# The decay of the smaller score blocks of pairs 8 to 15: added by VectorE from broadcast rows, in place of a TensorE product

## The chip, the cores and the metric

The kernel runs on one core of a Trainium2 chip. Its time is the device time of one execution in microseconds (us). Three executions of the kernel before took 973.07, 972.63 and 972.79 us, median 972.79. The profile is one more execution, recorded by the hardware profiler; it took 974.05 us by the clock that times the runs, and the span between its first and last instruction is 972.2 us.

The engines run side by side, each through its own list of instructions in order: TensorE (PE, with its weight loads as PEld), VectorE (DVE), ScalarE (ACT), GpSimd (POOL) and SyncE (SP), which here only starts DMA transfers.

## The reference

Attention over 4 batches of 8 heads, 576 positions and 64 dimensions a head, with a bias that decays with the distance of two positions, and then two dense layers with an activation between:

```python
scores = scale * np.matmul(q, k.transpose(0, 1, 3, 2))
causal = np.triu(np.ones((S, S), dtype=bool), k=1)
cum = np.cumsum(np.maximum(s, 0.0), axis=-1)
bias = -(cum[:, :, :, None] - cum[:, :, None, :])
scores = np.where(causal, -1000000000.0, scores + np.minimum(bias, 0.0))
attn = softmax(scores)          # max, exp, sum and divide, by rows
x = attn @ v                    # heads side by side: 2304 x 512
h = x @ w_in;  x = np.maximum(0.01 * h, h) @ w_out
h = x @ w_in2; out = (np.maximum(h, 0) + np.log1p(np.exp(-np.abs(h)))) @ w_out2
```

All of it is fp32. For a query at row i and a key at column j the bias is cum[j] - cum[i]: a value of the key's column less a value of the query's row.

## The kernel before, in words

The 32 heads are worked on as 16 pairs, p = 0 to 15; "the ninth pair" is p = 8. A pair's two heads (j = 0 and 1) lie on SBUF partitions 0 to 63 and 64 to 127, so that the score products of both stand side by side in the PE array. The 576 queries of a head are cut into four blocks of 128, t = 0 to 3, and a tail of 64. Block t sees (t + 1) * 128 keys. A pair is worked through in four units, in this order:

- A: block 3, 512 keys.
- B: the tails of both heads, 288 keys each. It takes its decay from the tile M, which `bias` (L267) has prepared.
- C: block 2, 384 keys.
- D: blocks 1 and 0, 256 and 128 keys.

For A, C and D, `scores` (L286) issues, for each block, a product K,Q and a second product BK,BQ into the same PSUM tile pt_s: BK and BQ hold the running sums, split in two parts, and rows of ones, and their product is the decay (L311). VectorE then reads the PSUM tile, adds the causal mask, and finds the row maximum in the same instruction (`maxima`, L332). ScalarE takes the exponential (L344), VectorE the reciprocal of the row sum (L350, L351), GpSimd multiplies by it (L355), TensorE transposes the result (L363 to L372), and after an evacuation by ScalarE or VectorE (L384, L386) TensorE multiplies by V (`pv`, L404).

The score tiles have the PSUM tags s0 and s1 (one for each head) with two buffers each. Units take the buffers in turn: A, B, C, D, and A of the next pair takes the buffers of C. So the first score products of the next pair wait until VectorE has finished the maxima of C, of head 0 for s0 and of head 1 for s1.

The order of all this is written by hand in one loop over steps n = 4p + i (L467). From p = 7 on (`late`), step i = 0 starts the scores of B and does the two products with V for the earlier pairs, step 2 starts the scores of C and D, step 3 those of the next pair's A. Between them `fill.step` puts pieces of the first dense layer of earlier batches on TensorE, so that it always has work. `later(n, ...)` issues an instruction n ticks on; a step has two ticks.

SyncE starts the transfers of a pair in step i = 0: V (of this pair, as soon as the product with V of p - 2 has read the old one), then Q, K, four small rows for BK and BQ, and the two loads for M of the next pair (`decays`, L253, from the sums c_d in DRAM). DMA transfers signal their end on eight semaphores in turn. A transfer whose semaphore still belongs to an unfinished one is not issued, and as SyncE works in order, nothing behind it is either.

`Fill` (L539 on) also loads and splits the weights of the first layer; raw weights land in the tiles rawi and rawo. After attention, the two dense layers run as one long chain of TensorE products (`ps_h` L145, `ps_out` L772).

Of the kernel before, what the change touches and what calls it, by code (L numbers as in the profile page):

```python
# [10 lines left out]
F32 = mybir.dt.float32  # L11
# [20 lines left out]
def attn_moe_moe(ctx, tc, q, k, v, s, w1i, w1o, w2i, w2o, out):  # L32
# [122 lines left out]
    def attention(att, ps, fills):  # L155
# [9 lines left out]
        M = two("M", [P, S])  # L165
        CQ, CD = (att.tile([P, n], F32, tag=nm, name=nm) for nm, n in (("CQ", 32), ("CD", 2 * TL)))
        V = two("V", [P, NB + 1, 2, D])
# [71 lines left out]
        def load(p, nm, queue=nc.sync, c=slice(None)):  # L239
            if p < NP:  # L240
                t, x = {"q": (Q, q), "k": (K, k), "v": (V, v)}[nm]
                queue.dma_start(t[p % 2][:, c], x[p, :, c])

        def rows(p):

            if p < NP:
                b, hs = heads(p)
                for j in range(2):
                    h, r = b * H + hs.start + j, j * D
                    move(BK[p % 2][r:r + 2], bb_d[h, :, :SB])  # L250
                    move(BQ[p % 2][r + 32:r + 34], bb_d[h, :, :SB])

        def decays(p):  # L253

            if p < NP:
                o = c_d.offset + p * 2 * S
                for j in range(2):
                    nc.sync.dma_start(M[p % 2][j * D:(j + 1) * D], bass.AP(c_d.tensor, o + j * S, [[0, D], [1, S]]))

        def columns():  # L260
            pt = ps.tile([P, 512], F32, tag="m", name="pt_c", bufs=1)
            nc.tensor.transpose(pt[:, :BH], CD[:BH], ident[:BH, :BH])
            for j in range(2):
                r = slice(j * D, (j + 1) * D)
                nc.vector.tensor_copy(CQ[r, :NP], pt[r, j:BH:2])

        def bias(p):  # L267
            if 0 < p < NP:
                m = M[p % 2]
                nc.vector.tensor_scalar(m, m, CQ[:, p:p + 1], None, op0=ALU.subtract)  # L270
                later(1, nc.gpsimd.tensor_tensor, m[:, SB:], m[:, SB:], maskl[:, SH - TL:], ALU.add)


        class Unit:
# [11 lines left out]
            def scores(self):  # L286
                i = self.p % 2
                bq, bk = (BQ[i], BK[i]) if self.p else (BQ0, BK0)
                ops = (Q[i], K[i]), (bq, bk)
                self.ps = [ps.tile([P, 512], F32, tag=f"s{j}", name="pt_s", bufs=2) for j in range(2)]  # L290
# [16 lines left out]
                for t, c in self.subs:  # L307
                    for x, y in ops:
                        for j in range(2):
                            r = slice(j * D, (j + 1) * D)  # L310
                            nc.tensor.matmul(  # L311
                                self.ps[j][:, c], x[r, t * P:(t + 1) * P], y[r, :(t + 1) * P],
                                start=x is Q[i], stop=x is bq,
                            )
# [4 lines left out]
            def maxima(self, j):  # L319
                if j == 0:  # L320
# [4 lines left out]
                w = slice(0, self.W)  # L325
                ml = (mask[:, w], maskl)[j] if not self.p else M[self.p % 2][:, j * SH:(j + 1) * SH]
                todo = [(w, ml, j)] if self.last else [
                    (c, mask[:, (NB - 1 - t) * P:], j * len(self.subs) + i) for i, (t, c) in enumerate(self.subs)
                ]
                low = self.stat(0, 0) if self.last and j else 3.0e38  # L330
                for c, m, e in todo:
# [126 lines left out]
        live = {}  # L458
        wide = 7

# [6 lines left out]
        for n in range(len(units) + 3):  # L467
# [27 lines left out]
            if i == 0:  # L495
                bias(p)
                if p:
                    load(p + 1, "q")
                    load(p + 1, "k")
                    rows(p + 1)  # L500
                    decays(p + 1)
            tick()
# [20 lines left out]
            if u2:  # L523
                if not soon:
                    u2.evacuate(0)
                u2.transpose(1)
            if i == 3 and not late:
                load(p + 1, "v")
# [7 lines left out]
    class Fill:  # L536
        def __init__(self, ps):
# [3 lines left out]
            self.stack = ExitStack()  # L541
            wio["i"] = new("rawi", 2)
            with_o = pool("rawo", 2, side="right")
# [4 lines left out]
            self.loads, self.splits = {}, {}  # L548
            for t, x in zip(at, zip(blocks, "iioiiiii" + "i" * 4)):
                for d, n in zip((self.loads, self.splits), t):  # L550
# [320 lines left out]
```

## Time and profile before

| | |
|---|---|
| Median of three executions | 972.79 us (972.63 to 973.07) |
| The profiled execution | 974.05 us, span 972.2 us |
| Attention | 0 to about 226 us of the span |
| Pairs 8 to 15 | about 105 to 226 us |
| VectorE, ScalarE, GpSimd busy, whole span | 526.8, 537.3, 576.5 us |

TensorE's share is in the rows below. Busy means that an instruction is being executed; a wait for a semaphore is not busy time. A row of the timeline stands for one instruction or for several like ones that follow on each other (x4 and so on); its second number is the time from the first one's start to the last one's end. A K,Q product in fp32 shows as two instructions for each head, so x4 for a pair.

### The profile page before, as it was taken

Reading aid. Unit: us, or ns where it says so; the run is one execution under the profiler, and the core shown is the slowest. Engines: PE = TensorE matmul, PEld = TensorE weight load, DVE = VectorE, ACT = ScalarE, POOL = GpSimd, SP = SyncE. Lnnn points to the kernel's source line nnn. Section 1 sums busy time; section 2 is a strip of 40 time slices with the busy share of each in tenths; the row PEclk is TensorE's granted clock in tenths of the full one; section 3 lists DMA queues with packets and bytes.
Section 4 is the critical chain, followed back from the end, with each engine's and each line's share of the span. In section 5 each row is a group of like instructions: output and inputs, shape, how many; then the busy total and the mean of one; then the engine's idle time right before and its main releaser. Section 6 shows DMA issues by size and latency. Waiting matters only on the chain.

```text
span 972.2 us, 14745 instructions
## 1 busy us (share of the span) xinstructions
PE 963.7 (99%) x5268; PEld 785.5 (81%) x5268; DVE 526.8 (54%) x1140; ACT 537.3 (55%) x1119; POOL 576.5 (59%) x568
## 2 busy tenths in 40 slices
PE   9999999999999999999999999999999999999998
PEld 6666767777988888888888888888888888888886
DVE  7888567553222232222234357667688768764434
ACT  6888677564453333333344457667656655654452
POOL 6778556443454444444445556777677767774554
PEclk9999999999999999999999999999999999999999
DMA  6544433421621111111111110211011201100202
GB/s 227 160 160 135 139 128 103 149 71 48 224 69 44 44 44 43 44 44 44 44 31 57 44 44 23 66 43 44 23 46 45 62 23 44 44 0 1 88 22 88
DMA packets 37774, 68.06 MB, mean 70 GB/s; under 512 B 3018, under 2 KB 20298, under 8 KB 37700
## 3 DMA queue, kind: packets, MB, share of 16 engines
q1 hardware_dynamic: 37268, 66.36, 21.2%
q8 instruction: 42, 0.69, 0.3%
q10 hardware_dynamic: 432, 0.75, 0.2%
q14 instruction: 32, 0.26, 0.1%
HBM read 59.01 MB, written 8.09 MB: 69 GB/s over the span
## 4 chain that ended last, share of the span: by engine, by line
PE 94%; DVE 3%; POOL 1%; ACT 1%; issue 1%; DMA 1%; SPq 0%; DVEq 0%; POOLq 0%
PE ps_h L145 40%; PE ps_out L772 37%; PE pt_s L311 4%; PE pt_t L372 3%; PE ps_o L631 3%; PE pt_v L404 3%; PE pt_s L404 1%; PE pt_t L367 1%; DVE sc L332 1%; PE pt_s L297 1%; PE pt_w L191 0%; POOL sc L355 0%; ACT sc L344 0%; DMA bb_d<-PA 0%; DVE PA L386 0%
## 5 line engine op out<-in xcount | busy, mean ns | idle before, releaser
L151 POOL TENSOR_TENSOR gl<-gf,gh 128x512 fp32r<-128x512 f32 (+2 forms) x148 | 182.8, 1236 | 151.2 <-ACT gh L150 141.5
L145 PE MATMUL ps_h<-xh,wih 128*128 128x512 f32 (+2 forms) x640 | 237.5, 371 | 0.0
L145 PE MATMUL ps_h<-xh,wil 128*128 128x512 f32 (+2 forms) x640 | 235.7, 368 | 0.0
L145 PE MATMUL ps_h<-xl,wih 128*128 128x512 f32 (+2 forms) x640 | 235.6, 368 | 0.0
L784 DVE TENSOR_TENSOR acc<-ps_out,acc 128x512 f32<-128x512 f32 (+1 forms) x115 | 73.8, 658 | 164.3 <-PE ps_out L772 164.3
L731 POOL TENSOR_TENSOR t<-e,t 128x512 f32<-128x512 f32 (+1 forms) x80 | 112.5, 1406 | 71.8 <-DVE t L730 71.1
L355 POOL TENSOR_SCALAR sc<-sc,st 128x512 f32<-128x512 f32 (+4 forms) x160 | 88.8, 566 | 80.3 <-DVE st L351 61.0
L145 PEld LDWEIGHTS ps_h<-xh,wil 128*128 128x128 f32 x640 | 120.5, 188 | 19.6
L145 PEld LDWEIGHTS ps_h<-xh,wih 128*128 128x128 f32 x640 | 120.6, 188 | 19.3
L145 PEld LDWEIGHTS ps_h<-xl,wih 128*128 128x128 f32 x640 | 120.6, 188 | 19.2
L715 ACT ACTIVATE gf<-ps_h 128x512 f32<-128x512 f32 (+2 forms) x68 | 37.3, 549 | 177.2 <-PE ps_h L145 174.4
L150 ACT ACTIVATE gh<-gf 128x512 fp32r<-128x512 f32 (+2 forms) x148 | 86.3, 583 | 49.1 <-DVE gf L741 48.4
L772 PE MATMUL ps_out<-woh,gl 128*128 128x512 f32 x289 | 112.5, 389 | 0.0
L772 PE MATMUL ps_out<-woh,gh 128*128 128x512 f32 x289 | 112.4, 389 | 0.0
L772 PE MATMUL ps_out<-wol,gh 128*128 128x512 f32 x289 | 112.4, 389 | 0.0
L123 POOL TENSOR_TENSOR wm<-wm,wt 128x512 int32<-128x512 int32 x64 | 85.3, 1333 | 30.7 <-DVE wm L120 30.7
L344 ACT ACTIVATE sc<-sc,st 128x512 f32<-128x512 f32 (+2 forms) x144 | 83.7, 584 | 35.2 <-DVE st L332 28.1
L772 PE MATMUL ps_out<-gh,wol 128*128 128x512 f32 (+2 forms) x272 | 99.1, 364 | 0.0
L772 PE MATMUL ps_out<-gh,woh 128*128 128x512 f32 (+2 forms) x272 | 99.1, 364 | 0.0
L772 PE MATMUL ps_out<-gl,woh 128*128 128x512 f32 (+2 forms) x272 | 99.0, 364 | 0.0
L730 DVE TENSOR_SCALAR t<-e 128x512 f32<-128x512 f32 (+1 forms) x80 | 44.1, 552 | 98.2 <-ACT e L721 98.2
L114 DVE TENSOR_SCALAR wm<-wm 128x512 f32<-128x512 f32 x64 | 39.0, 610 | 93.4 <-ACT wm L108 93.3
(118 smaller groups left out, 1674.9 us busy)
## 6 DMA issues: line engine op xcount, KB each, us to landing
rawi<-in_moe_w_in SPq DMA_DIRECT2D x32, 512.0 KB
rawo<-in_moe_w_out SPq DMA_DIRECT2D x32, 512.0 KB
K<-in_k SPq DMA_DIRECT2D x15, 432.0 KB
V<-in_v SPq DMA_DIRECT2D x16, 320.0 KB
Q<-in_q SPq DMA_DIRECT2D x15, 320.0 KB
out<-acc SPq DMA_DIRECT2D x17, 256.0 KB
M<-c_d SPq DMA_DIRECT2D x30, 144.0 KB
part<-o SPq DMA_DIRECT2D x12, 256.0 KB
```

Source lines behind the costliest of these rows:

```text
L114: nc.vector.tensor_scalar(mf, mf, D_MIN, D_MAX, op0=ALU.max, op1=ALU.min)
L123: nc.gpsimd.tensor_tensor(m, m, t, op=ALU.add)
L145: nc.tensor.matmul(ps, a, b, start=kk == 0 and n == 0, stop=kk == KD - 1 and n == 2)
L150: nc.scalar.activation(gh, gf, AF.Copy)
L151: nc.gpsimd.tensor_tensor(gl, gf, gh.bitcast(F32), op=ALU.subtract)
L311: nc.tensor.matmul(self.ps[j][:, c], x[r, t * P:(t + 1) * P], y[r, :(t + 1) * P], start=x is Q[i], stop=x is bq,)
L344: nc.scalar.activation(x, x, AF.Exp, scale=-1.0, bias=self.stat(0, e + self.last), accum_out=self.stat(1, e))
L355: nc.gpsimd.tensor_scalar(x, x, self.stat(2, e), 1.0, op0=ALU.mult, op1=ALU.mult)
L730: nc.vector.tensor_scalar(t, e, 1.0, -1.0, op0=ALU.add, op1=ALU.add)
L731: nc.gpsimd.tensor_tensor(t, e, t, op=ALU.subtract)
L772: nc.tensor.matmul(u, a, v, start=f == 0 and m == 0, stop=f == G - 1 and m == 2 and j == k - 1)
L784: nc.vector.tensor_tensor(d[..., x], o[..., x], d[..., x], op=ALU.add)
```

## The change

For p = 8 to 15 the product BK,BQ of the units C and D is left out (`soft`); unit A keeps it. What it gave is added by VectorE with the maximum: the operand that was the causal mask is now a tile that holds, for every query row and key column, the bias itself, and on the diagonal block the mask too.

That tile is called `slope`. It is built from rows of the sums that a DMA copies to all 128 partitions (`spread`), and from a column CN with the negative sums of the query block (`ramp`): for the last 128 columns VectorE adds column and mask to the row in one instruction, for the columns ahead of them GpSimd adds the column. There is one such tile for each head and block: for t = 2 and for head 0 of t = 1 they lie in a tile that takes the place of one of the two buffers for raw weights, for the rest in M[1]. Therefore the M of unit B is M[0] in all of these pairs (`gap`), and its load for the next pair is moved from step 0 to step 2, behind the last use. The rows for t = 2 are loaded in step 3 of the pair ahead, those for t = 1 and 0 in step 0 behind Q, K, BK and BQ; `ramp` for t = 2 stands in step 0 and for t = 1 and 0 in step 2, between the maxima of C for head 0 and for head 1. CN is made once at the start from three more transposes.

```diff
@@ -163,7 +163,8 @@
         Q, K = two("Q", [P, ZQ]), two("K", [P, ZK])
         BQ, BK = two("BQ", [P, SB], F32R), two("BK", [P, SB], F32R)
         M = two("M", [P, S])
-        CQ, CD = (att.tile([P, n], F32, tag=nm, name=nm) for nm, n in (("CQ", 32), ("CD", 2 * TL)))
+        CQ, CN, CD = (att.tile([P, n], F32, tag=nm, name=nm) for nm, n in (("CQ", 32), ("CN", 96), ("CD", 2 * TL)))
+        wide = 7
         V = two("V", [P, NB + 1, 2, D])
 
         PA = att.tile([P, 2, NB, P + TL], F32, tag="PA", name="PA")
@@ -241,6 +242,39 @@
                 t, x = {"q": (Q, q), "k": (K, k), "v": (V, v)}[nm]
                 queue.dma_start(t[p % 2][:, c], x[p, :, c])
 
+        def soft(p):
+            return wide < p < NP
+
+        def gap(p):
+            return M[0 if soft(p) else p % 2]
+
+        ramps = []
+
+        def slope(t, j):
+            if not ramps:
+                ramps.append(wio["j"].tile([P, 2 * DM], F32, tag="raw", name="slope"))
+            x, y = ramps[0], M[1]
+            a = ((y, 2 * P + j * P), ((x, 6 * P), (y, 0))[j], (x, 3 * P * j))[t]
+            return a[0][:, a[1]:a[1] + (t + 1) * P]
+
+        def spread(p, ts):
+            if soft(p):
+                for t in ts:
+                    n = (t + 1) * P
+                    for j in range(2):
+                        x = bass.AP(c_d.tensor, c_d.offset + (2 * p + j) * S, [[0, P], [1, n]])
+                        nc.sync.dma_start(slope(t, j), x)
+
+        def ramp(p, ts):
+            if soft(p):
+                for t in ts:
+                    for j in range(2):
+                        m, k = slope(t, j), t * B * H + 2 * p + j
+                        col, d = CN[:, k:k + 1], m[:, t * P:]
+                        nc.vector.scalar_tensor_tensor(d, d, col, mask[:, SB - P:], op0=ALU.add, op1=ALU.add)
+                        if t:
+                            nc.gpsimd.tensor_scalar(m[:, :t * P], m[:, :t * P], 1.0, col, op0=ALU.mult, op1=ALU.add)
+
         def rows(p):
 
             if p < NP:
@@ -255,7 +289,7 @@
             if p < NP:
                 o = c_d.offset + p * 2 * S
                 for j in range(2):
-                    nc.sync.dma_start(M[p % 2][j * D:(j + 1) * D], bass.AP(c_d.tensor, o + j * S, [[0, D], [1, S]]))
+                    nc.sync.dma_start(gap(p)[j * D:(j + 1) * D], bass.AP(c_d.tensor, o + j * S, [[0, D], [1, S]]))
 
         def columns():
             pt = ps.tile([P, 512], F32, tag="m", name="pt_c", bufs=1)
@@ -263,10 +297,13 @@
             for j in range(2):
                 r = slice(j * D, (j + 1) * D)
                 nc.vector.tensor_copy(CQ[r, :NP], pt[r, j:BH:2])
+            for t in range(NB - 1):
+                nc.tensor.transpose(pt[:, (t + 1) * BH:(t + 2) * BH], c1[:, t * P:(t + 1) * P], ident[:BH, :BH])
+            nc.vector.tensor_scalar(CN, pt[:, BH:NB * BH], -1.0, None, op0=ALU.mult)
 
         def bias(p):
             if 0 < p < NP:
-                m = M[p % 2]
+                m = gap(p)
                 nc.vector.tensor_scalar(m, m, CQ[:, p:p + 1], None, op0=ALU.subtract)
                 later(1, nc.gpsimd.tensor_tensor, m[:, SB:], m[:, SB:], maskl[:, SH - TL:], ALU.add)
 
@@ -286,7 +323,8 @@
             def scores(self):
                 i = self.p % 2
                 bq, bk = (BQ[i], BK[i]) if self.p else (BQ0, BK0)
-                ops = (Q[i], K[i]), (bq, bk)
+                self.soft = soft(self.p) and not self.last and self.ts[0] < NB - 1
+                ops = ((Q[i], K[i]), (bq, bk))[:2 - self.soft]
                 self.ps = [ps.tile([P, 512], F32, tag=f"s{j}", name="pt_s", bufs=2) for j in range(2)]
                 if self.last:
 
@@ -310,7 +348,7 @@
                             r = slice(j * D, (j + 1) * D)
                             nc.tensor.matmul(
                                 self.ps[j][:, c], x[r, t * P:(t + 1) * P], y[r, :(t + 1) * P],
-                                start=x is Q[i], stop=x is bq,
+                                start=x is Q[i], stop=x is ops[-1][0],
                             )
 
             def stat(self, k, e, n=1):
@@ -323,10 +361,12 @@
                     if self.last:
                         self.sc = view(self.sc, 0, [self.W, 2], [1, self.W])
                 w = slice(0, self.W)
-                ml = (mask[:, w], maskl)[j] if not self.p else M[self.p % 2][:, j * SH:(j + 1) * SH]
+                ml = (mask[:, w], maskl)[j] if not self.p else gap(self.p)[:, j * SH:(j + 1) * SH]
                 todo = [(w, ml, j)] if self.last else [
                     (c, mask[:, (NB - 1 - t) * P:], j * len(self.subs) + i) for i, (t, c) in enumerate(self.subs)
                 ]
+                if self.soft:
+                    todo = [(c, slope(t, j), e) for (t, _), (c, _, e) in zip(self.subs, todo)]
                 low = self.stat(0, 0) if self.last and j else 3.0e38
                 for c, m, e in todo:
                     nc.vector.tensor_tensor_reduce(
@@ -456,7 +496,6 @@
         order = [[NB - 1], [], [NB - 2], [1, 0]]
         units = [(p, ts) for p in range(NP) for ts in order]
         live = {}
-        wide = 7
 
         def start(n):
             if n < len(units) and n not in live:
@@ -498,6 +537,13 @@
                     load(p + 1, "q")
                     load(p + 1, "k")
                     rows(p + 1)
+                    if p < wide:
+                        decays(p + 1)
+                    spread(p, (1, 0))
+                    ramp(p, (2,))
+            if i == 2:
+                ramp(p, (1, 0))
+                if p >= wide:
                     decays(p + 1)
             tick()
             if n == len(units):
@@ -524,6 +570,8 @@
                 if not soon:
                     u2.evacuate(0)
                 u2.transpose(1)
+            if i == 3:
+                spread(p + 1, (2,))
             if i == 3 and not late:
                 load(p + 1, "v")
             elif p and not late and i in ((0, 2) if p < NP else (1, 2)):
@@ -539,14 +587,14 @@
             self.units = []
             new = lambda nm, bufs=1: self.stack.enter_context(pool(nm, bufs, side="right"))
             self.stack = ExitStack()
-            wio["i"] = new("rawi", 2)
+            wio["i"], wio["j"] = new("rawi"), new("rawj")
             with_o = pool("rawo", 2, side="right")
             wio["o"] = with_o.__enter__()
 
             blocks = [(f, nm) for nm in "io" for f in range(G)] + [(G + f, nm) for f in range(2) for nm in "io"]
             at = (-2, 3), (-1, 9), (1, 13), (6, 17), (11, 19), (19, 21), (21, 23), (23, 25), (28, 31), (33, 36), (38, 41), (43, 46)
             self.loads, self.splits = {}, {}
-            for t, x in zip(at, zip(blocks, "iioiiiii" + "i" * 4)):
+            for t, x in zip(at, zip(blocks, "ijoijiji" + "i" * 4)):
                 for d, n in zip((self.loads, self.splits), t):
                     d.setdefault(n, []).append(x)
```

Three places show the new order, all in the pair p = 11. The first is SyncE's list in step 0. Each row names the DMA semaphore of its own transfer (DMAHW and a number), whose last transfer must have landed; V_98, K_87, M_94 and so on are the buffers. Before:

```order
L242 DMA V_98<-in_v 128x640 [waits DMAHW3_49,PE_49]
L242 DMA Q_85<-in_q 128x640 [waits DMAHW4_49]
L242 DMA K_87<-in_k 128x864 [waits DMAHW5_49]
L82 DMA BK_91<-bb_d 2x512 [waits DMAHW6_49]
L82 DMA BQ_89<-bb_d 2x512 [waits DMAHW7_49]
L82 DMA BK_91<-bb_d 2x512 [waits DMAHW0_49]
L82 DMA BQ_89<-bb_d 2x512 [waits DMAHW1_49]
L258 DMA M_93<-c_d 64x576 [waits DMAHW2_49,DVE_49]
L258 DMA M_93<-c_d 64x576 [waits DMAHW3_49]
```

Now:

```order
L243 DMA V_99<-in_v 128x640 [waits DMAHW7_49,PE_49]
L243 DMA Q_85<-in_q 128x640 [waits DMAHW0_49]
L243 DMA K_87<-in_k 128x864 [waits DMAHW1_49]
L82 DMA BK_91<-bb_d 2x512 [waits DMAHW2_49]
L82 DMA BQ_89<-bb_d 2x512 [waits DMAHW3_49]
L82 DMA BK_91<-bb_d 2x512 [waits DMAHW4_49]
L82 DMA BQ_89<-bb_d 2x512 [waits DMAHW5_49]
L266 DMA slope<-c_d 128x256 [waits DMAHW6_49,DVE_49]
L266 DMA M_94<-c_d 128x256 [waits DMAHW7_49,DVE_49]
L266 DMA M_94<-c_d 128x128 [waits DMAHW0_49]
L266 DMA M_94<-c_d 128x128 [waits DMAHW1_49,DVE_49]
```

The two loads of M for the next pair are gone from here. In their place stand four loads: the rows of t = 1 for head 0 (slope) and head 1 (M_94), and of t = 0 for both heads. The last three share the semaphores of V, Q and K just ahead of them.

The second place is VectorE in step 2, from the maxima of C on (ISA is the instruction of L332, which the trace calls CUSTOM_DVE_ANT_0, and the read of its accumulator). Before:

```order
L351 RECIPROCAL st<-st 128x1 [waits DVE_49]
L332 ISA sc,st<-pt_s,mask 128x384 [waits PE_49,Pool_49]
L332 ISA st 128x1
L332 ISA sc,st<-pt_s,mask 128x384 [waits PE_49]
L332 ISA st 128x1
L114 TENSOR_SCALAR wm<-wm 128x512 [waits Activation_49]
L332 ISA sc,st<-pt_s,mask 128x256 [waits PE_49,Pool_49]
```

Now:

```order
L391 RECIPROCAL st<-st 128x1 [waits DVE_49]
L372 ISA sc,st<-pt_s,slope 128x384 [waits PE_49,Pool_49]
L372 ISA st 128x1
L274 SCALAR_TENSOR_TENSOR slope<-slope,CN,mask 128x128 [waits DMAHW6_49]
L274 SCALAR_TENSOR_TENSOR M_94<-M_94,CN,mask 128x128 [waits DMAHW7_49]
L274 SCALAR_TENSOR_TENSOR M_94<-M_94,CN,mask 128x128 [waits DMAHW0_49]
L274 SCALAR_TENSOR_TENSOR M_94<-M_94,CN,mask 128x128 [waits DMAHW1_49]
L372 ISA sc,st<-pt_s,slope 128x384 [waits PE_49]
```

Between the maxima of C for the two heads stand four additions, each behind the landing of its own load.

The third place is TensorE's last work of step 2 and the first of step 3, where the scores of A of the next pair begin. Before:

```order
L372 MATMUL pt_t<-ident,sc 128x128 [waits DVE_49,Pool_49]
L372 MATMUL pt_t<-ident,sc 128x128 x3
L311 MATMUL pt_s<-K_87,Q_85 128x512 [waits DMAHW1_49,DMAHW0_49,DVE_49]
L311 MATMUL pt_s<-K_87,Q_85 128x512 [waits DVE_49]
L311 MATMUL pt_s<-BK_91,BQ_89 128x512 [waits DMAHW3_49,DMAHW2_49]
```

Now:

```order
L412 MATMUL pt_t<-ident,sc 128x128 [waits DVE_49,Pool_49]
L412 MATMUL pt_t<-ident,sc 128x128 x3
L349 MATMUL pt_s<-K_87,Q_85 128x512 [waits DMAHW1_49,DMAHW0_49,DVE_49]
L349 MATMUL pt_s<-K_87,Q_85 128x512 [waits DVE_49]
L349 MATMUL pt_s<-BK_91,BQ_89 128x512 [waits DMAHW3_49,DMAHW2_49]
```

Nothing moved here: the product for head 0 waits for VectorE (maxima of C, head 0), that for head 1 again (head 1), and what is left out ahead are the six products BK,BQ of C and D.

## Rows read from the trace of the kernel before

**Rows 1.** Page, part 1: busy time of each engine, share, instructions.
```profile
PE 963.7 (99%) x5268; PEld 785.5 (81%) x5268; DVE 526.8 (54%) x1140; ACT 537.3 (55%) x1119; POOL 576.5 (59%) x568
```

**Rows 2.** TensorE's waits, 115 to 227 us: total us, times, longest.
```profile
PE pt_t L372 <- ACT PB L384: 0.3, 1, 0.3
```

**Rows 3.** Timeline of PE, pair 11, step 2: start us, us, what.
```profile
161.62 0.92 PE L311 MATMUL pt_s<-K,Q 64*128 64x384 f32 x4
162.08 0.63 PE L311 MATMUL pt_s<-BK,BQ 64*128 64x384 f32 x2
162.54 0.60 PE L311 MATMUL pt_s<-K,Q 64*128 64x256 f32 x4
...
163.47 0.66 PE L372 MATMUL pt_t<-ident,sc 128*128 128x128 f32 x4
...
165.90 1.13 PE L311 MATMUL pt_s<-K,Q 64*128 64x512 f32 x4
```

**Rows 4.** Chain that ended last, second dense layer: start us, us, what.
```profile
360.86 2.72 PE ps_out L772 x12
```

**Rows 5.** Waits of SyncE, 112 to 119.5 us, pair 8.
```profile
SPq L636 <- DMA K<-in_k: 1.7, 1, 1.7
```

**Rows 6.** Waits of SyncE, 128 to 135 us, pair 9.
```profile
SPq L242 <- DMA K<-in_k: 1.7, 1, 1.7
SPq L93 <- DMA Q<-in_q: 0.4, 1, 0.4
```

**Rows 7.** Waits of SyncE, 142 to 148 us, pair 10.
```profile
SPq L242 <- DMA K<-in_k: 1.4, 1, 1.4
```

**Rows 8.** Timeline of SyncE, pairs 8 to 11 and 14: start us, issue time us.
```profile
112.34 0.33 SPq L242 DMA_DIRECT2D V<-in_v  x1
...
116.08 0.59 SPq L98 DMA_DIRECT2D rawo<-in_moe_w_out  x1
...
128.07 0.33 SPq L242 DMA_DIRECT2D V<-in_v  x1
128.46 0.42 SPq L242 DMA_DIRECT2D Q<-in_q  x1
...
132.17 0.41 SPq L93 DMA_DIRECT2D rawi<-in_moe_w_in  x1
...
142.12 0.36 SPq L242 DMA_DIRECT2D V<-in_v  x1
...
146.15 0.36 SPq L98 DMA_DIRECT2D rawo<-in_moe_w_out  x1
...
157.50 0.36 SPq L242 DMA_DIRECT2D V<-in_v  x1
...
203.94 0.36 SPq L242 DMA_DIRECT2D V<-in_v  x1
```

**Rows 9.** Timeline of SyncE and PEld near the start, pair 1's small rows.
```profile
14.72 0.24 SPq L82 DMA_DIRECT2D BQ<-bb_d  x1
...
16.25 0.18 PEld L311 LDWEIGHTS pt_s<-BK,BQ 64*128 64x128 f32 x1 [0.45 <-DMA BQ<-bb_d]
```

**Rows 10.** Timeline of DVE, pairs 10 and 11.
```profile
148.52 0.54 DVE L117 TENSOR_SCALAR wm<-wm 128x512 int32<-128x512 int32 x1
...
151.07 0.29 DVE L332 CUSTOM_DVE_ANT_0 sc<-pt_s,mask 128x128 f32<-128x128 f32 x1
...
163.30 0.56 DVE L332 CUSTOM_DVE_ANT_0 sc<-pt_s,mask 128x384 f32<-128x384 f32 x1
```

**Rows 11.** Timeline of PE: the first score product after pairs 8, 9, 10, 14.
```profile
121.07 1.13 PE L311 MATMUL pt_s<-K,Q 64*128 64x512 f32 x4
...
135.12 1.13 PE L311 MATMUL pt_s<-K,Q 64*128 64x512 f32 x4
...
150.50 1.13 PE L311 MATMUL pt_s<-K,Q 64*128 64x512 f32 x4
...
212.31 1.13 PE L311 MATMUL pt_s<-K,Q 64*128 64x512 f32 x4
```

## The prediction

> **What bounds the kernel now.** I read the page's busy times first: TensorE is busy for 963.7 of 972.2 us, the next engine for 59% [rows 1]. Then the waits of TensorE in the stretch of the change, pairs 8 to 15: two, 0.3 us and 0.2 us in 112 us, the longer one shown [rows 2]. So here TensorE sets the time, and what is taken off its list is gained, as long as the work is delivered to it in time; a wait put into its list is lost in full, since the dense layers behind it run without a gap and cannot give it back. Hence two questions: what do the removed products cost, and is anything that TensorE waits for now later than TensorE. For the second I read the timelines of TensorE, VectorE and SyncE around step 2 of a pair, and the waits of SyncE.
>
> **What is removed.** In each of 8 pairs six products BK,BQ (two heads; 384, 256 and 128 keys). The one over 384 keys holds 0.46 us between its start and the next [rows 3]; at that rate per key the 768 keys cost 0.92 us a pair. That is an upper end: a start is stamped while the K,Q product ahead is still streaming. The scores of C and D take 163.47 - 161.62 = 1.85 us in all [rows 3]. A dense product of 512 columns takes 2.72 / 12 = 0.227 us [rows 4], so 768 columns in one pass, both heads side by side, are 0.34 us. If K,Q makes four such passes (1.36 us), the five make 1.70 of the 1.85 us. I take 0.35 us a pair, bounds 0.34 and 0.92.
>
> **What is added on TensorE.** Three small transposes at the start, near 0.1 us each by width; they stand where TensorE also waits for the first rows (it idles for loads near 16 us [rows 9]), so 0 to 0.3 us. I take 0.2.
>
> **What is added elsewhere.** VectorE gets two additions of 128 columns in step 0 and four in step 2 of each pair, GpSimd two of 256 and two of 128 columns. No row shows this very instruction; the nearest on VectorE with two tensors and 128 columns takes 0.29 us [rows 10]. In step 0 they have cover: in the same stretch VectorE and GpSimd wait for TensorE's transposes, and the rows for t = 2 are asked for in the pair before. If that cover were gone it would cost the maxima of A up to 0.6 us, which no product waits for until C of the same pair. GpSimd's additions in step 2 stand ahead of the second half of B's scaling, whose transposes come only after A's next scores; I cost them at nothing.
>
> Step 2 is different. The four additions stand between the maxima of C for head 0 and for head 1, and the first score product of the next pair needs the latter. In pair 11 the maxima for head 0 start at 163.30 and take 0.56 us [rows 10]; TensorE needs those of head 1 at 165.90 [rows 3]. Four additions of 0.29 us alone would fit. What counts is when their rows land.
>
> **The loads.** The transfers take eight semaphores in turn, and one whose semaphore is in use is not issued. That bites before the change already: counted from V, Q is second and K third; the tenth transfer (rawi) waits for Q and the eleventh (V or part) for K [rows 5 to 7]. Now the four new loads are number eight to eleven, and the last, t = 0 of head 1, is the eleventh: it cannot be issued before K has landed. When does K land? In pair 8 SyncE finishes rawo at 116.08 + 0.59 and waits 1.7 us: 118.37. In pair 9, 132.17 + 0.41 + 1.7 = 134.28. In pair 10, 146.15 + 0.36 + 1.4 = 147.91 [rows 5 to 8]. That is 6.03, 6.21 and 5.79 us after the issue of V (112.34, 128.07, 142.12), mean 6.01. The moved loads of M stood behind K, so this does not change.
>
> How long from issue to landing for a load of 64 KB that finds the queues nearly empty? No row shows it. From below: the 4 KB row issued at 14.72 is waited for until 16.25, so 1.5 us [rows 9]. From above: Q, with V ahead of it, was issued at 128.46 and held rawi until 132.17, so 3.7 us [rows 6, 8]. I take the middle, 2.6.
>
> [...]
>
> So after the change the next pair's scores can go on no earlier than K's landing plus 2.6 (load), 0.29 (last addition), 0.56 (maxima) and some 0.03 for hand-over: K + 3.48 us. Against the starts before:
> - Pair 8: 118.37 + 3.48 = 121.85, before 121.07 [rows 11]: +0.78.
> - Pair 9: 134.28 + 3.48 = 137.76, before 135.12 [rows 11]: +2.64. Its step 0 had less fill work, so its scores come only 7.05 us after V instead of 8.4.
> - Pair 10: 147.91 + 3.48 + 0.54 = 151.93, before 150.50 [rows 11]: +1.43. A weight step of 0.54 us [rows 10] stands between the additions and the maxima.
> - Pair 11: 157.50 + 6.01 + 3.48 = 166.99, before 165.90 [rows 3, 8]: +1.09.
> - Pairs 12 to 14: as the last of them, 203.94 + 9.49 = 213.43, before 212.31 [rows 8, 11]: +1.12 each, 3.36.
> - Pair 15: no next pair, so no Q and K; its loads are early and it gains 0.35.
>
> The removed products do not help in pairs 8 to 14: TensorE only reaches the wait 0.35 us sooner. The sum is 9.30 - 0.35 + 0.20 = +9.15 us. On the profiled execution that is 974.05 + 9.15 = 983.2; this one stands 1.26 us over the median of the timed runs, and on that median, 972.79, it is 981.9 us. A load of 1.5 us takes 1.1 off seven times: +1.45 us, 974.2. One of 3.7 us adds as much: +16.9, 989.6.
>
> What is queued behind: the four additions hold VectorE from about 163.9 to the last landing, and behind them stand the maxima of D and the reciprocals of C. The next pair's B takes D's buffers, but only after A's scores and a piece of fill work, so I cost it at nothing; with the weight steps among them (pairs 8 to 11) least is left over (rival 3).
>
> **Rivals.**
> 1. The rows are there in time: faster. Then 8 pairs gain 0.35 us: 2.8 - 0.2 = 2.6, 970.2 us; by the upper price 8 x 0.92 - 0.2 = 7.2, 965.6 us. For it: in step 0 and pair 15 this holds, and the engines have time to spare. Against it: the last load must land within 8.05 us of V (8.4 less the 0.35 gained) less 0.88 for addition, maxima and hand-over, 7.2; issue alone is at 6.0, and even the 4 KB row took 1.5. It needs a load of under 1.2 us, or K 1 us earlier.
> 2. The wait just eats the gain: no change. With a load of 1.4 us pairs 8 and 11 to 14 come out near their old times and pair 9 alone costs over 1 us; about 973.5. For it: the lower bound is near. Against it: that bound was 4 KB in two rows, not 128.
> 3. Later still: VectorE comes so late that B of the next pair also waits for D, in the pairs with weight steps, and late landings of one of the 16 DMA engines add to it. Another 1 us in seven pairs: 989. For it: the time from V to K's landing already differs by 0.4 us between pairs. Against it: ahead of the last load stand only small ones once K has landed.
>
> **How the numbers follow.** Forecast 0.66, rival 1 0.13, rival 2 0.10, rival 3 0.11. Within 0.2% (1.95 us) no change can be told from none. Faster takes rival 1: 0.13. The same takes rival 2 and the low end of the forecast: 0.12. Slower: 0.75. The likeliest time is 981.9; its own range is 974.2 to 989.6. The range given reaches down to 973.5, over most of rival 2, and leaves out rival 1 and part of rival 3, together under 0.2.
>
> **What the new profile would show.** In pairs 8 to 14 TensorE waits in step 3, in front of or within the K,Q product over 512 keys, for the maxima of C, about 1.4 us a pair (1.1 and the 0.35 gained) and about 3 in pair 9. VectorE idles in front of its fourth addition, released by a load of M. SyncE waits for K in front of the fourth new load. C and D take about 1.5 us instead of 1.85. Pair 15 shows no such wait. I am wrong if the fourth load is issued without a wait for K, if it lands within 1.2 us, or if the scores of the next pair start on time.

## The result, and the profile after

The kernel after takes 986.68 us (median of four runs, 985.6 to 990.43) against 972.86 us before (972.63 to 973.07): ratio 1.015, 95% interval 1.0137 to 1.0162, so 13.8 us slower. The forecast was 981.9 us, range 973.5 to 989.6.

The page's busy times of the kernel after answer to [rows 1]:

```profile
PE 970.3 (99%) x5223; PEld 786.2 (80%) x5223; DVE 548.7 (56%) x1189; ACT 537.6 (55%) x1119; POOL 590.5 (60%) x600
```

45 products are fewer, 48 dropped and three transposes added, and yet TensorE counts 6.6 us more as busy, so its busy time does not tell what the kernel lost. The waits tell more. Those of TensorE, 100 to 245 us, answer to [rows 2] (total us, times, longest):

```profile
PE pt_s L349 <- DVE st L372: 2.7, 5, 1.0
PE pt_s L349 <- DMA M<-c_d: 2.3, 2, 1.5
PE pt_t L407 <- ACT PA L424: 1.7, 1, 1.7
```

L349 is the score product. Six of the seven waits in the first two rows stand in front of A's K,Q product for head 1, which needs the buffer that C's maxima (L372) empty; the seventh, 0.2 us, stands in front of C. The second row has a DMA as its releaser, but in the order of the instructions this product waits for VectorE: the load only landed at nearly the same time. The third row is in pair 15, and nothing in the prediction stands for it.

SyncE's waits in 105 to 240 us, and VectorE's in front of the additions (L274):

```profile
SPq L266 <- DMA K<-in_k: 8.4, 7, 1.6
```

```profile
DVE M L274 <- DMA M<-c_d: 7.1, 9, 1.4
```

Seven times, once in each pair with a next K, a load of rows (L266) waits for K to land: the fourth new load behind its semaphore. How that runs on is seen in pair 10. SyncE's timeline (start, issue time), then the chain of waits (start, us), then VectorE's timeline:

```profile
146.64 0.33 SPq L243 DMA_DIRECT2D V<-in_v  x1
...
147.50 0.42 SPq L243 DMA_DIRECT2D K<-in_k  x1
...
152.03 0.32 SPq L266 DMA_DIRECT2D M<-c_d  x1
```

```profile
152.03 3.15 DMA M<-c_d
```

```profile
152.55 0.56 DVE L372 CUSTOM_DVE_ANT_0 sc<-pt_s,slope 128x384 f32<-128x384 f32 x1
153.03 0.40 DVE L274 SCALAR_TENSOR_TENSOR slope<-slope,CN,mask 128x128 f32<-128x128 f32 x1
153.36 0.84 DVE L274 SCALAR_TENSOR_TENSOR M<-M,CN,mask 128x128 f32<-128x128 f32 x2
155.20 0.75 DVE L274 SCALAR_TENSOR_TENSOR M<-M,CN,mask 128x128 f32<-128x128 f32 x1 [1.01 <-DMA M<-c_d]
155.87 0.41 DVE L117 TENSOR_SCALAR wm<-wm 128x512 int32<-128x512 int32 x1
156.21 0.54 DVE L372 CUSTOM_DVE_ANT_0 sc<-pt_s,slope 128x384 f32<-128x384 f32 x1
```

The fourth load is issued at 152.03, lands 3.15 us later at 155.18, the last addition starts at 155.20, and behind it come a weight step and C's maxima for head 1. TensorE's timeline shows the product behind them, which answers to 150.50 in [rows 11]:

```profile
156.82 0.69 PE L349 MATMUL pt_s<-K,Q 64*128 64x512 f32 x1 [1.00 <-DVE st L372]
```

What was removed stands in the same view for pair 15: the scores of C and D take 236.42 - 234.92 = 1.50 us, before 1.85 [rows 3].

```profile
234.92 1.57 PE L349 MATMUL pt_s<-K,Q 64*128 64x384 f32 x12
236.42 0.66 PE L412 MATMUL pt_t<-ident,sc 128*128 128x128 f32 x4
```

Now the whole stretch, by the time from the first product of one pair's A to that of the next (all worked out from such rows of TensorE's timeline, in us). A pair's wait stands within the next pair's A, so it shows in the interval one to the right; e1, e3, e8 and e9 are experiments told of below.

| interval of pair | 8 | 9 | 10 | 11 | 12 | 13 | 14 |
|---|---|---|---|---|---|---|---|
| before | 15.74 | 14.05 | 15.38 | 15.40 | 15.65 | 15.40 | 15.36 |
| after | 15.72 | 14.99 | 19.28 | 17.35 | 16.88 | 16.60 | 16.36 |
| e1, additions later | 15.71 | 13.88 | 15.69 | 16.13 | 15.67 | 15.04 | 15.03 |
| e3, products left out | 15.71 | 13.88 | 15.04 | 15.02 | 15.69 | 15.02 | 15.04 |
| e8, rows kept | 15.72 | 15.61 | 16.44 | 17.16 | 15.70 | 15.59 | 15.44 |
| e9, from pair 12 | 15.71 | 14.05 | 15.40 | 15.39 | 15.28 | 15.05 | 15.12 |

After less before is +10.2 over the seven intervals; from A of pair 15 to the end it is 762.8 against 759.9, +2.9. Together 13.1. Ahead of pair 8 the profile of the kernel after is 0.6 us the earlier one, so the spans differ by 12.5; the medians differ by 13.8 because the profiled execution of before took 1.2 us more than the median of its runs.

Two things in it were foreseen by no step. In the interval of pair 10 (from 135.41 on) TensorE's granted clock fell. The windows view of the kernel after (stretch, length, busy us of the five engines, granted clock, DMA share, GB/s):

```profile
136.00:138.20 2.20, 0.65 (x4) 0.13 (x3) 1.68 (x5) 0.15 (x1) 1.05 (x2) 1.00 0.67 206
138.20:139.90 1.70, 1.70 (x8) 0.90 (x9) 1.25 (x10) 1.70 (x5) 0.56 (x2) 0.91 1.00 352
139.90:142.70 2.80, 2.80 (x9) 2.03 (x8) 0.69 (x1) 2.11 (x9) 1.84 (x3) 0.50 0.23 58
142.70:145.00 2.30, 2.30 (x26) 1.41 (x26) 1.59 (x6) 1.49 (x4) 0.50 (x2) 0.94 0.00 0
```

TensorE did little from 136.0 to 138.2, worked on at full clock, and then ran at 0.50: in the whole third stretch and, by the means of 0.91 and 0.94, for 0.3 us on either side of it, 3.4 us in all. Its timeline tells the price, beside the same steps at full clock behind pair 14:

```profile
138.07 0.69 PE L349 MATMUL pt_s<-K,Q 64*128 64x512 f32 x1 [1.55 <-DMA M<-c_d]
...
139.39 0.92 PE L407 MATMUL pt_t<-ident,sc 128*128 128x128 f32 x4
139.96 0.78 PE L145 MATMUL ps_h<-xh,wih 128*128 128x512 f32 x1
...
143.02 0.47 PE L335 MATMUL pt_s<-K,Q 64*64 64x288 f32 x4
...
225.12 0.63 PE L407 MATMUL pt_t<-ident,sc 128*128 128x128 f32 x4
...
227.18 0.71 PE L335 MATMUL pt_s<-K,Q 64*64 64x288 f32 x8
```

From the transposes to B's scores: 143.02 - 139.39 = 3.63 us against 227.18 - 225.12 = 2.06, so 1.6 us. Not every run pays it: the timed run of 985.6 us has a mean granted clock of 1.000, the other three have 0.995 to 0.998, and the profiled one 0.998.

The other is pair 15, which has no next pair and no late rows. VectorE's timeline, TensorE's, and TensorE's of the kernel before:

```profile
237.08 0.40 DVE L274 SCALAR_TENSOR_TENSOR slope<-slope,CN,mask 128x128 f32<-128x128 f32 x1
237.40 1.34 DVE L274 SCALAR_TENSOR_TENSOR M<-M,CN,mask 128x128 f32<-128x128 f32 x3
238.67 0.55 DVE L372 CUSTOM_DVE_ANT_0 sc<-pt_s,slope 128x384 f32<-128x384 f32 x1
```

```profile
240.59 0.63 PE L407 MATMUL pt_t<-ident,sc 128*128 128x128 f32 x4 [1.69 <-ACT PA L424]
```

```profile
228.16 0.63 PE L367 MATMUL pt_t<-ident,sc 128*128 128x128 f32 x4 [0.39 <-ACT PA L384]
```

Four additions without a wait still take 238.67 - 237.08 = 1.59 us and push C's maxima for head 1 back. ScalarE takes the exponential of C (its row starts at 239.26) in front of the evacuation into PA (L424, 239.87), in order, and so TensorE's transposes of the next unit wait 1.69 us instead of 0.39.

### The profile page after: what moved, and what is told of

Same layout as the page of the kernel before. It is cut to its first block, busy times and chain, and to the rows that moved or that the text cites. A ratio compares the mean times of both kernels' runs of the same rounds, so it can differ in the third digit from the quotient of the medians.

```text
span 984.7 us, 14824 instructions
## 1 busy us (share of the span) xinstructions
PE 970.3 (99%) x5223; PEld 786.2 (80%) x5223; DVE 548.7 (56%) x1189; ACT 537.6 (55%) x1119; POOL 590.5 (60%) x600
## 4 chain that ended last, share of the span: by engine, by line
PE 91%; DVE 3%; DMA 3%; POOL 1%; issue 1%; ACT 0%; SPq 0%; DVEq 0%; POOLq 0%
PE ps_h L145 39%; PE ps_out L820 37%; PE pt_s L349 4%; PE pt_v L444 3%; PE ps_o L679 2%; PE pt_t L412 2%; DMA M<-c_d 2%; PE pt_s L444 1%; DVE sc L372 1%; PE pt_t L407 1%; PE pt_s L335 1%; PE pt_w L192 0%; POOL sc L395 0%; DMA Q<-in_q 0%; DMA part<-o 0%
```

## The experiments

The theory: the additions for t = 1 and 0 stand ahead of C's maxima for head 1 and wait for rows that land late, so the next pair's scores are late. Rivals to it: the removed products or the semaphores' order, the load's own time, the clock, or the additions' length. The runs of before beside the experiments had medians of 972.63 to 972.79 us.

**e1: the additions behind C's maxima for head 1.** GpSimd's two additions move with the four of VectorE; the loads stay as they are.

```diff
             if i == 2:
-                ramp(p, (1, 0))
...
+            if i == 2:                  # behind u1.maxima(1)
+                ramp(p, (1, 0))
```

> The changed kernel with one move: the additions for t = 1 and 0 (VectorE's four and GpSimd's two) stand behind the maxima of C for head 1 in place of ahead of them. Theory A (the whole loss is the next pair's scores waiting for the maxima of C behind the late fourth load): the wait is gone, D's maxima come later but still ahead of the next pair's B; the six products a pair are gained, 8 x 0.35 us: about 970.5 us (969.5 to 973). Rival B (the extra loads and additions cost by their amount, wherever they stand): stays above 980 us.

973.73 us, ratio 1.0011 (1.0002 to 1.0021), 0.7 us above the expected range. Of 13.8 us 0.9 are left, though SyncE's list is the same and it waits for K as often:

```profile
SPq L266 <- DMA K<-in_k: 9.5, 7, 1.8
```

So the place of the additions is the cause. What is left stands in the intervals of pairs 10 and 11 (table: 15.69 and 16.13, in e3 15.04 and 15.02). TensorE's timeline of e1 has in them two rows of B, and one that spans C and D, that last longer than in e3:

```profile
139.67 1.34 PE L335 MATMUL pt_s<-K,Q 64*64 64x288 f32 x8
...
155.36 1.03 PE L335 MATMUL pt_s<-K,Q 64*64 64x288 f32 x8
...
163.47 2.17 PE L349 MATMUL pt_s<-K,Q 64*128 64x384 f32 x12
```

The same rows of e3:

```profile
137.18 0.72 PE L298 MATMUL pt_s<-K,Q 64*64 64x288 f32 x8
...
152.23 0.71 PE L298 MATMUL pt_s<-K,Q 64*64 64x288 f32 x8
...
159.96 1.57 PE L312 MATMUL pt_s<-K,Q 64*128 64x384 f32 x12
```

0.62 + 0.32 + 0.60 = 1.54 of the 1.76 us between e1 and e3 in these two intervals. B takes the buffers of D, whose maxima now stand behind the additions; that is the first two. In the third, D takes the buffers of B: B's maxima for head 1 start only at 164.14, 0.86 us behind the end of a product of GpSimd that ran from 162.00 to 163.28. That this product held VectorE back is not shown.

**e2: the loads of these rows ahead of Q and K.**

```diff
+                    spread(p, (1, 0))
                     load(p + 1, "q")
                     load(p + 1, "k")
                     rows(p + 1)
-                    spread(p, (1, 0))
```

> The changed kernel with the four loads of rows for t = 1 and 0 issued ahead of Q and K (behind V), the additions left where they are. Theory A: no wait for K, rows land in time, but four additions of 0.42 us still stand between the maxima of C: pair 8 gains, pairs 9 to 14 lose 0.1 to 0.7 us each, pair 15 0.9 us: about 974.6 us (973 to 977). Rival C (the loads alone are the loss, the additions are hidden): 970.2 us. Rival B: above 980 us.

980.91 us, ratio 1.0084 (1.0069 to 1.0099): far above the theory's range, and in that of rival B, though not for its reason. The rows are early, but now K is late. TensorE's waits in this kernel, 100 to 245 us, and one of K's loads in its chain:

```profile
PE pt_s L349 <- DMA K<-in_k: 3.8, 4, 1.6
PE pt_s L349 <- DVE wm L117: 2.5, 1, 2.5
```

```profile
130.46 5.63 DMA K<-in_k
```

The second row names a weight step, which this product does not read. C's maxima are done 2.1 us before the product starts, so a late K is the likely cause here too, but no row shows it. In the kernel after the rows, asked for last, come late; here it is K.

**e3: the kernel before without the products BK,BQ of C and D in pairs 8 to 15**, and nothing in their place.

```diff
-                ops = (Q[i], K[i]), (bq, bk)
+                few = 7 < self.p and not self.last and self.ts[0] < NB - 1
+                ops = ((Q[i], K[i]), (bq, bk))[:2 - few]
...
```

> The kernel before without the products BK,BQ of the units C and D in pairs 8 to 15 and nothing in their place (the decay of those blocks is left out). The price of the products alone: 8 x 0.35 = 2.8 us by one pass in five, 970.1 us; by the starts in the timeline 8 x 0.92 = 7.4 us, 965.5 us.

971.29 us, ratio 0.9985 (0.9975 to 0.9994). All that could be won here is 1.5 us, not the 2.8 that 8 x 0.35 makes: in the table pairs 10, 11, 13 and 14 gain 0.32 to 0.38, pair 9 0.17, pairs 8 and 12 nothing, and in pair 15 the gain turns into a wait of TensorE for ScalarE, 0.75 us instead of 0.39.

```profile
225.46 0.63 PE L368 MATMUL pt_t<-ident,sc 128*128 128x128 f32 x4 [0.75 <-ACT PA L385]
```

**e4: the kernel after with these products issued again**, so that the decay counts twice there.

```diff
-                ops = ((Q[i], K[i]), (bq, bk))[:2 - self.soft]
+                ops = (Q[i], K[i]), (bq, bk)
...
```

> The changed kernel with the products BK,BQ of C and D issued again (the decay of those blocks is counted twice). Theory A: TensorE reaches the same wait 0.35 us later, so pairs 8 to 14 take as long as in the changed kernel: 986.7 us (986 to 988). Rival (TensorE's work adds up and the wait is short of it): 2.8 us more, 989.5 us.

988.92 us, ratio 1.0168 (1.0152 to 1.0183), 2.2 us over the kernel after and nearer to the second expectation. But the intervals of the two ratios overlap (1.0152 to 1.0183 and 1.0137 to 1.0162), so it is not shown that the products cost anything where TensorE waits behind them. If they do, one way is that they delay C's maxima, with which VectorE's chain of additions begins. The two profiles do not settle it, since in this one the clock fell behind another pair:

```profile
192.00:194.00 2.00, 2.00 (x7) 1.78 (x8) 0.90 (x4) 1.99 (x9) 0.99 (x2) 0.50 0.21 65
```

**e5: the rows of t = 0 of both heads in one load.** The last of the rows is then the tenth transfer and waits for Q, not for K. (The new call of `slope` only makes the tile.)

```diff
+                slope(2, 0)
                 for t in ts:
                     n = (t + 1) * P
+                    if t == 0:
+                        x = bass.AP(c_d.tensor, c_d.offset + 2 * p * S, [[0, P], [S, 2], [1, n]])
+                        nc.sync.dma_start(M[1][:, 2 * P:4 * P].rearrange("p (j x) -> p j x", x=P), x)
+                        continue
```

> The changed kernel with the rows of t = 0 for both heads in one load, so that the last of the new loads is the tenth from V on and waits for Q (landed 3.3 to 4.1 us after V) and no longer for K (4.8 to 5.7 us). Theory A (the semaphore that K holds sets the issue of the last load): its issue 1.3 to 2 us earlier, and the time falls to near that of the kernel with all rows ahead of Q and K, about 976 us (974.5 to 979). Rival (the load is late because the queues are full, not because it is issued late): within 2 us of the changed kernel, above 984.5 us.

988.23 us, ratio 1.0154 (1.0138 to 1.017): what the rival expected, and the theory did not. The load is issued earlier, in pair 13 2.88 us behind K; in pair 10 of the kernel after it was 4.53 (152.03 - 147.50 above):

```profile
198.88 0.42 SPq L243 DMA_DIRECT2D K<-in_k  x1
...
201.76 0.37 SPq L267 DMA_DIRECT2D M<-c_d  x1
```

But it takes longer. In the chain the loads of these rows in pairs 10, 11 and 13:

```profile
149.39 3.95 DMA M<-c_d
...
168.20 4.11 DMA M<-c_d
...
201.76 5.07 DMA M<-c_d
```

3.95 to 5.07 us instead of 3.15, with twice the bytes, and with K still on its way. The wait for K's semaphore, on which the prediction built, is real, but taking it away this way wins nothing. TensorE's product behind it, in pairs 10 and 13:

```profile
155.87 0.69 PE L354 MATMUL pt_s<-K,Q 64*128 64x512 f32 x1 [1.16 <-DVE st L377]
...
207.99 0.69 PE L354 MATMUL pt_s<-K,Q 64*128 64x512 f32 x1 [0.81 <-DVE st L377]
```

In pair 13 the longer load is the limit: it lands at 201.76 + 5.07 = 206.83, and the product starts 1.16 us later. In pair 10 the load is not all: it lands at 149.39 + 3.95 = 153.34, and the product starts 2.53 us later, where in the kernel after it was 156.82 - 155.18 = 1.64. What took the 0.89 more, with two additions behind the load instead of one, no row here shows.

**e6: pair 9 as before**, the other seven as after.

```diff
         def soft(p):
-            return wide < p < NP
+            return wide < p < NP and p != 9
         def gap(p):
-            return M[0 if soft(p) else p % 2]
+            return M[0 if wide < p < NP else p % 2]
```

> The changed kernel with the pair 9 left as in the kernel before (its products, no rows). Theory A with the clock: the wait in pair 9 (2.7 us against the kernel before) and the half clock behind it (six products of 512 columns at 0.43 in place of 0.23 us, and the transposes next to them, 1.4 us) both go: about 982.6 us, and no stretch near 140 us with a granted clock of 0.5. Rival (the half clock comes from the kernel's other gaps too): only the wait goes, 984 us, and a stretch at 0.5 shows in another place.

983.88 us, ratio 1.0118 (1.0101 to 1.0135), 2.8 us less than after. The interval of pair 10 falls from 19.28 to 15.04 us, by 4.2, and some of that comes back in later pairs. The time is the rival's, 984, yet the granted clock of this profile is 1.00 from 105 to 240 us: here the half clock went with pair 9's wait. That it went in every run is not shown: one of the four timed runs has a mean clock of 0.998, as the profile of the kernel after has.

**e7: e1 and e2 together.** Both edits as above.

> Both moves together: rows for t = 1 and 0 loaded ahead of Q and K, additions behind the maxima of C for head 1. Theory A: no wait is left that TensorE meets; the products' 2.8 us are gained, 970 us (969.3 to 971.5), at most 1 us below the kernel with the additions moved alone. Rival (Q and K, now loaded later, are late for the next pair's scores): above 973 us, with waits of TensorE for DMA Q or K.

980.83 us, ratio 1.0077 (1.0055 to 1.0098), as the rival had it: TensorE waits four times for K, 2.1 us in all, as in e2. The theory had counted e2's loads as free.

**e8: the rows of t = 1 and 0 loaded in pair 8 alone and kept**; the additions stay in their place.

```diff
         def spread(p, ts):
-            if soft(p):
+            if soft(p) and (p == wide + 1 or ts == (2,)):
```

> The kernel after, but the rows of t = 1 and 0 are loaded in pair 8 alone and kept: pairs 9 to 15 add their columns to what lies there (so the decay of those blocks is that of pair 8 plus what adds up). The four additions stay where they are on VectorE, between C's maxima, and wait for no load in pairs 9 to 15; the four loads leave SyncE's list. Theory A (the wait for the late rows is the loss): only pair 8 keeps its wait of 1 us or so, and pair 15 its 1.3 us for the four additions in a row; the rest is near the kernel with the additions moved later, about 975 us (973.5 to 976.5). Rival B (four additions of 0.4 us in that place are the loss by themselves, because they push back C's second maxima and ScalarE's evacuation behind them, as in pair 15): 1 to 1.3 us a pair in eight pairs, about 982 us (980 to 984), with TensorE waiting for ScalarE's evacuation instead of for the maxima.

979.21 us, ratio 1.0073 (1.0059 to 1.0086): between the two expectations. 6.6 of the 13.8 us are still lost, and the table says where. Pair 8 still waits for late rows, and the interval of pair 9, in which that wait stands, is 1.56 over before. Behind it no row is late any more. The intervals of pairs 12, 13 and 14 (waits of pairs 11 to 13) are back to 0.05, 0.19 and 0.08 over before: there the rows were the loss. Those of pairs 10 and 11 are 1.06 and 1.76 over before, and pair 15 keeps its wait of 1.69: there the additions themselves are. The worst is pair 10, VectorE's timeline and GpSimd's:

```profile
150.41 0.40 DVE L274 SCALAR_TENSOR_TENSOR slope<-slope,CN,mask 128x128 f32<-128x128 f32 x1
150.74 1.35 DVE L274 SCALAR_TENSOR_TENSOR M<-M,CN,mask 128x128 f32<-128x128 f32 x3
152.01 1.48 DVE L117 TENSOR_SCALAR wm<-wm 128x512 int32<-128x512 int32 x1
153.41 0.55 DVE L372 CUSTOM_DVE_ANT_0 sc<-pt_s,slope 128x384 f32<-128x384 f32 x1
```

```profile
151.91 1.29 POOL L662 TENSOR_TENSOR gl<-gf,gh 128x512 fp32r<-128x512 f32 x1
```

1.6 us of additions push the weight step beside a product of GpSimd that ends at 153.20, and there it takes 1.48 us instead of 0.54 [rows 10]: 0.94 us more, and an end 0.29 us behind GpSimd's. In the kernel after, where the late rows hold this step back until 155.87, behind such a product that ends at 155.80, it took 0.41 us. The 0.54 of the kernel before stand beside another step of GpSimd, a scaling from 148.28 to 149.43. No run changed this by itself, so that the product beside it is the cause is likely, but not shown.

**e9: e1's order, and the whole change from pair 12 on**, so that pairs 8 to 11, with the weight steps, stay as before.

```diff
-        wide = 7
+        wide, from_12 = 7, 11
         def soft(p):
-            return wide < p < NP
+            return from_12 < p < NP
...
-                    if p < wide:
+                    if p < from_12:
                         decays(p + 1)
...
-                if p >= wide:
+                if p >= from_12:
                     decays(p + 1)
```

> The kernel with the additions moved behind C's second maxima, and the whole change (products left out, rows, additions, M[0] alone) from pair 12 on instead of pair 8, so the pairs with weight steps (8 to 11) stay as before. Theory A (in pairs 10 and 11 the weight steps on VectorE were what the later additions collided with, 1.8 us in all; pairs 13 to 15 gain 0.35 us each and pair 12 nothing, as without the products): 972.86 - 1.05 = 971.8 us, plus 0.2 for the transposes: 972.0, ratio 0.999. Rival B (whatever pairs it covers, waits for late rows eat the gain): 973 to 974, ratio 1.000 to 1.001.

972.26 us (before beside it 972.64), ratio 0.9995 (0.9987 to 1.0004): no difference that can be told. In the table pairs 12 to 14 gain 0.37, 0.35 and 0.24 us. The first expectation had three such gains, but in pairs 13 to 15. Pair 15 gains nothing: at its end TensorE waits 0.74 us for ScalarE instead of 0.39. No version here that adds the decay beats the kernel before beyond its interval; e3 bounds what one could win.

## Why the prediction was right, and where its sizes were off

The sign, the place and the mechanism held: TensorE waits in A's K,Q product for C's maxima, these wait behind the additions, and the fourth of those for a load that is issued when K has landed. e1 shows that the place of the additions is the cause. By its own steps (the measured losses are after less before in the table, one interval on; each already has taken off the 0.35 that the next pair's scores are shorter):

| | forecast | measured |
|---|---|---|
| pair 8 | +0.78 | +0.94 |
| pair 9 | +2.64 | +3.90, of it 1.6 at half clock |
| pair 10 | +1.43 | +1.95 |
| pair 11 | +1.09 | +1.23 |
| pairs 12, 13 | +1.12 each | +1.20, +1.00 |
| pairs 14 and 15 together | +1.12 - 0.35 | +2.93 |

- The removed products: 1.85 to 1.50 us, the 0.35 taken. That 8 x 0.35 = 2.8 us could be won, as rival 1 had it, is refuted: e3 wins 1.5.
- K's landing: 5.79 us after V was taken for pair 10; it was 152.03 - 146.64 = 5.39. Over the seven pairs the fourth load was issued 4.8 to 6.0 us after V, where the mean taken was 6.01. Why K landed earlier in most of them was not tried.
- The load: 2.6 us taken, 3.15 measured in pair 10, in the bounds of 1.5 and 3.7. The 0.55 more and K's earlier landing, 0.40, nearly cancel in this pair.
- The addition: 0.29 taken from a row that reads PSUM. The groups by line and shape of the kernel after (ns: min/median/max) give a median of 0.46:

```profile
L274 DVE SCALAR_TENSOR_TENSOR slope<-slope,CN,mask x24: 352/455/568, 109.7 to 237.1; 128x128 f32<-128x128 f32 x24
L274 DVE SCALAR_TENSOR_TENSOR M<-M,CN,mask x24: 339/456/1366, 118.4 to 238.2; 128x128 f32<-128x128 f32 x24
```

- "Four additions of 0.29 us alone would fit" failed. In pair 15 they cost 1.3 us of wait where a gain of 0.35 was forecast, and by e8, with the rows there, they still cost 1.06 us in pair 9 and 1.76 in pair 10, the latter with a weight step that takes 0.94 longer in its new place. Only in pairs 11 to 13 are the late rows nearly all of it. Where two causes run side by side the later one sets the time, and the earlier shows only when the later is gone: the prediction saw the later one alone.
- The half clock behind pair 9, 1.6 us, was in no term.
- Rivals: 1 had the kernel faster if the rows are there in time. e8 has them there from pair 9 on without late Q and K and is still 6.6 us slower than before, only 1.56 of it at pair 8's late rows, so rows in time were not enough in this order. Rival 2 needed a load of 1.4 us; it was 3.15. Rival 3 (B waits for D) shows in no wait of the kernel after, but in e1 it makes 0.94 of the 1.76 us that are left in two intervals. No view shows when a single one of the DMA engines lands its part, which was the rest of that rival.

Of the last row 1.30 us are pair 15's (1.69 - 0.39), so pair 14 lost 1.63. Without the half clock pairs 8 to 14 come to 0.94 + 2.30 + 1.95 + 1.23 + 1.20 + 1.00 + 1.63 = 10.25 against 9.30: the terms were 0.95 short in all, the clock 1.6 and pair 15 1.65 (1.30 and the missing 0.35). 9.15 + 0.95 + 1.6 + 1.65 = 13.35; the runs differ by 13.8. The 9.15 holds 0.2 for the three transposes, which no run shows by itself; in the kernel after they take 0.37 us together at 11.93 (L301), behind a wait of 0.45 for VectorE. The 0.03 for hand-over was the author's estimate; in pair 10 of the kernel after the last addition starts 0.02 us behind the landing, at 155.20. The forecast of 981.9 is 4.8 us under the measured 986.68. The clock, which was in no term, and pair 15, whose term had the other sign, make 3.25 of it. The range that holds the result was drawn for the load's time and not for these two, so that it reaches far enough is in part luck.

## What to carry to other kernels

Before work goes on an engine that is half idle, look at which of its instructions the busy engine waits for, and put the new work behind it: here that alone was worth 12.9 of 13.8 us. A saving on the bound engine counts only in pairs or stages where the next-latest engine has that much room, so leave the work out once without replacement (e3) to see what can be won at all. And when a wait is found, try it away with the data already there (e8): what is then still lost is the next cause.

## What the runs showed of the hardware

- A wait can cost more than itself, but need not: after about 1.6 us of idle TensorE in pair 9 the granted clock fell to 0.50 for 3.4 us, and that cost 1.6 us. After the wait of 1.69 us in pair 15 it did not fall, nor after one of 2.46 us in e2 (the mean granted clock of that execution is 1.0). What tells them apart no run shows.

```profile
240.60:242.00 1.40, 1.40 (x9) 1.22 (x10) 1.00 (x5) 1.40 (x6) 1.10 (x2) 1.00 0.00 0
242.00:244.00 2.00, 2.00 (x20) 1.28 (x18) 0.54 (x3) 1.25 (x5) 0.47 (x2) 1.00 0.00 0
```

- A load of 64 KB issued once K had landed took 3.15 us to land in pair 10; one of 128 KB issued while K was still on its way took 3.95 to 5.07 us (e5).
- A step of VectorE that took 0.54 us in pair 10 of the kernel before took 1.48 us there in e8, beside a product of two tensors on GpSimd of 1.29 us.
